# Converting float64 weights on the fly: a mask that also sets a bit, and the sign put into the power, in a recurrence with an MLP

## The chip, the cores and the metric

The kernel runs on one core of a Trainium2 chip. The metric is the device time of one execution in microseconds. The core has five engines with instruction streams of their own, each in program order: TensorE (PE in the profile; its weight loads are PEld), VectorE (DVE), ScalarE (ACT), GpSimd (POOL) and SyncE (SP), which here mostly issues DMA transfers. They wait for one another by semaphores.

## The reference

Two blocks, one after the other. The first is a recurrence over 768 steps for 4 batches and 8 heads with a state of 40 x 40; the second an MLP whose activation is h cos h:

```
for t in range(S):
    y[:, :, t] = np.einsum('bhd,bhde->bhe', rt, state)
    Sa = np.einsum('bhde,bhe->bhd', state, at)
    state_decay = state * wt[:, :, None, :] - np.einsum('bhd,bhe->bhde', Sa, bt)
    state = state_decay + np.einsum('bhd,bhe->bhde', vt, kt)
...
x = attn_out.transpose(0, 2, 1, 3).reshape(B * S, H * D)    # 3072 x 320
h = x @ w_in                                                # 320 x 2048
g = h * np.cos(h)
return (g @ w_out).astype(np.float32)                       # 2048 x 320
```

The inputs of the recurrence are float32. The two weights of the MLP come as float64, since a float32 array times a float64 scalar gave that in the set-up. [...]

## The kernel before, in words

**The recurrence** is worked in 24 chunks of 32 steps (`NCH`), with the four batches on the 128 partitions. For each chunk there is preparation of the decays (`p1_w`, `p1_a`, `p1_b`, `p1_n`), an inverse of a small triangular matrix for every group of four chunks (for the first eight chunks by blocks, `pair_first`, `pair_second`), preparation of keys, values and queries (`p2_in`, `p2_kn`, `p2_v`, `p2_k`, `p2_g`) and the chain from state to state (`main`: `ch_t`, `ch_q`, `ch_x`, `ch_s`, `ch_z`). `ch_z` ends with four pairs of VectorE operations (qz L738, yt L745), four products on GpSimd (qz L739) and one more (yt L750). The yt tile goes to DRAM and comes back transposed as xT (`tokens`, L759 to L771).

**The MLP** runs over pairs of chunks, 256 tokens each, in pieces: `first_a` and `first_b` multiply xT with w_in into ph, L812 to L822 form the cosine and the product gT, `second` multiplies gT with w_out into po.

**The order** of all this is written out by hand. `step` emits one segment, then those works put off with `later` that have come due, then a stated number of entries of two lists: `inv_steps` (the inverse) and `w_steps` (the weights). Each engine executes what it was given in just this order. Where TensorE would fall idle early in the kernel, `busy` and `kept_busy` put matmuls of zeros (tiles busy, spare).

**The weights** are cut into 20 pieces of 128 x 512 values: 8 of w_in_sb, 2 of w_in_tail and 10 of w_out_sb. Each piece has four works, made by `rounded`:

- `fetch` (L233 to L237) loads the piece as pairs of 32-bit words into a tile `words`, low word first, high word second, so either word is read with a stride of two. The tile shares the buffers of other things (gT, nt, u, inv).
- `taken` (L239 to L249): VectorE masks the upper 20 bits of the mantissa out of the high word (mant, L243) and shifts the exponent down (expo, L244). ScalarE moves the exponent to its float32 place with Relu (L247) and takes the sign of the high word (sign, L249).
- `mantissa` (L251 to L256): VectorE adds the low word times 2^-32 to the masked bits (L253). ScalarE brings the sum to a fraction with the leading 1 and a constant factor by Identity with a scale and a bias (L256).
- `product` (L258 to L262): VectorE multiplies fraction and power (the exponent's bits read as float32) into the weight's place (L259). GpSimd multiplies that with the sign (L262).

The constant factors fold 1/(2 pi) into w_in and 2 pi into w_out; they are held per partition in by_in and by_out.

The list `w_steps` is built at L921 to L930: first `taken` of pieces 0 and 1 and `mantissa` of piece 0, and then for every piece n its `product`, the `fetch` of a later piece, `mantissa` of n + 1 and `taken` of n + 2. So `taken` of a piece comes ahead of the product of the piece before it, and mant, expo and sign have two buffers each (pool `sb2`). The list is emptied between 48 and 143 us: two or four entries beside a segment for chunks 0 and 1, then two or three; a piece of the MLP that needs weights not yet converted takes further entries first (`piece`, L1020).

Of the kernel before, what the change touches and what calls it, by code (L numbers as in the profile page):

```python
# [9 lines left out]
F32 = mybir.dt.float32  # L10
I32 = mybir.dt.int32
U32 = mybir.dt.uint32
ALU = mybir.AluOpType
ACTF = mybir.ActivationFunctionType
# [6 lines left out]
def kernel(  # L21
# [43 lines left out]
    nc = tc.nc  # L65
    B, H, S, D = r.shape
    P, C, DP = 128, 32, 64
# [12 lines left out]
    const = ctx.enter_context(tc.tile_pool(name="const", bufs=1))  # L80
    ring = ctx.enter_context(tc.tile_pool(name="ring", bufs=7))
    sb1 = ctx.enter_context(tc.tile_pool(name="sb1", bufs=1))
    sb2 = ctx.enter_context(tc.tile_pool(name="sb2", bufs=2))
# [6 lines left out]
    def kept(name, shape, n=1, fill=None, part=lambda t: t, on=nc.gpsimd):  # L90

        tiles = []
        for i in range(n):
            t = const.tile(shape, F32, tag=f"{name}{i}", name=f"{name}{i}")
            if fill is not None:
                on.memset(part(t), fill)
            tiles.append(t)
        return tiles
# [8 lines left out]
    src = {"r": r, "k": k, "v": v, "w": w, "a": a, "b": b}  # L107
# [12 lines left out]
    for n, fill in (("w", 1.0), ("a", 0.0), ("b", 0.0)):  # L120
        for i in range(4):
            x = slice((i - 2) * H * DP, (i - 1) * H * DP)
            if i < 2:
                t = const.tile([P, H, DP], F32, tag=f"nat_{n}{i}", name=f"nat_{n}{i}")
            else:
                t = {
                    "w": w_in_sb[:, 0, late:], "a": w_in_sb[:, 1, late:], "b": late_out
                }[n][:, x].rearrange("p (h d) -> p h d", h=H)
# [4 lines left out]
    for n in "kvr":  # L133
        t = const.tile([P, H, D], F32, tag=f"nat_{n}", name=f"nat_{n}")
# [71 lines left out]
        nc.gpsimd.memset(bn_b[i][:, :, C // 2 : C], 0.0)  # L206
    kn_b = kept("kn", [P, H, DP], 2, 0.0, padding)

    by_in = kept("by_in", [P, 1], 1, 0.5 / math.pi)[0]
    by_out = kept("by_out", [P, 1], 1, 2.0 * math.pi)[0]  # L210
    to_bits = kept("to_bits", [P, 1], 1, (127.0 - 1023) * 2**23)[0]


# [5 lines left out]
    WID = 512  # L219
    first_done, second_done = [], []  # L220

    def rounded(m, dst, src, by, by_sb):

        pool, tag = (
            ((sb2, "gT"), (sb2, "gT"), (sb1, "nt"), (sb1, "u"), (sb1, "inv"))[m % 5]
            if m < 10 else ((sb1, "nt"), (sb1, "u"), (sb1, "inv"))[(m - 10) % 3]
        )
        t = {}  # L230

        def fetch():
            t["words"] = pool.tile([P, WID, 2], I32, tag=tag, name="words")  # L233
            for rows, cols, part in src:
                nc.sync.dma_start(
                    t["words"][rows, cols].rearrange("p n w -> p (n w)"), part.bitcast(I32)
                )  # L237

        def taken():  # L239
            hi = t["words"][:, :, 1]  # L240
            t["mant"] = sb2.tile([P, WID], I32, tag="mant", name="mant")
            t["expo"] = sb2.tile([P, WID], I32, tag="expo", name="expo")
            nc.vector.tensor_scalar(t["mant"], hi, 0xFFFFF, None, ALU.bitwise_and)  # L243
            nc.vector.tensor_scalar(  # L244
                t["expo"], hi, 20, 0x7FF, ALU.logical_shift_right, ALU.bitwise_and
            )
            nc.scalar.activation(t["expo"], t["expo"], ACTF.Relu, bias=to_bits, scale=2.0**23)  # L247
            t["sign"] = sb2.tile([P, WID], mybir.dt.bfloat16, tag="sign", name="sign")
            nc.scalar.activation(t["sign"], hi, ACTF.Sign)  # L249

        def mantissa():  # L251
            frac = t["mant"].bitcast(F32)
            nc.vector.scalar_tensor_tensor(  # L253
                frac, t["words"][:, :, 0].bitcast(U32), 2.0**-32, t["mant"], ALU.mult, ALU.add
            )
            nc.scalar.activation(frac, frac, ACTF.Identity, bias=by_sb, scale=2.0**-20 * by)  # L256

        def product():  # L258
            nc.vector.tensor_tensor(  # L259
                dst, t["mant"].bitcast(F32), t["expo"].bitcast(F32), ALU.mult  # L260
            )
            nc.gpsimd.tensor_tensor(dst, dst, t["sign"], ALU.mult)  # L262

        return fetch, taken, mantissa, product

    def weights():


        wide = moe_w_in.dtype != F32
        work = []  # L270

        def put(dst, src, by, by_sb):
            if wide:
                work.append(rounded(len(work), dst, src, by, by_sb))
                return

            def fetch():
                for rows, cols, part in src:
                    nc.sync.dma_start(dst[rows, cols], part)

            none = lambda: None
            work.append((fetch, none, none, lambda: nc.scalar.mul(dst, dst, by)))

        flat_out = w_out_sb.rearrange("p f n -> p (f n)")
        for j in range(NF // 4):
            cs = slice(j * WID, (j + 1) * WID)
            for i in range(2):
                put(
                    w_in_sb[:, i, cs], [(every, slice(0, WID), moe_w_in[i * P : (i + 1) * P, cs])],
                    0.5 / math.pi, by_in,  # L290
                )
            if j % 2 == 0:
                put(
                    w_in_tail[:, j : j + 2].rearrange("p j f n -> p (j f n)"),
                    [
                        (
                            full[e], slice(2 * i * P, 2 * (i + 1) * P),
                            moe_w_in[2 * P :, (4 * (j + i) + 2 * e) * P : (4 * (j + i) + 2 * e + 2) * P],
                        )
                        for i in range(2)  # L300
                        for e in range(2)
                    ],
                    0.5 / math.pi, by_in,
                )
            first_done.append(len(work))
            for o in range(0, NF * DM, WID):
                if not 4 * j * DM <= o < 4 * (j + 1) * DM:
                    continue
                parts = []
                for f in range(o // DM, (o + WID - 1) // DM + 1):  # L310
                    lo, hi = max(o, f * DM), min(o + WID, (f + 1) * DM)
                    parts.append(
                        (
                            every, slice(lo - o, hi - o),
                            moe_w_out[f * P : (f + 1) * P, lo - f * DM : hi - f * DM],
                        )
                    )
                put(flat_out[:, o : o + WID], parts, 2.0 * math.pi, by_out)
            second_done.append(len(work))
        return work  # L320

# [582 lines left out]
    def main(c):  # L904
        def last():
            ch_z(c)
            if c + 2 < NCH:
                later(8 if c == 2 else 1, lambda: p2_kn(c + 2))

        return [lambda: ch_t(c), lambda: ch_q(c), lambda: ch_x(c), lambda: ch_s(c), last]  # L910

    with tc.manual_schedule():

        w_work = weights()
        w_count = [0]

# [116 lines left out]
        for c in range(NCH):  # L1033
            t, q, x, s, z = main(c)
# [116 lines left out]
```

## Time and profile before

| | us |
|---|---|
| median of 4 runs | 809.18 (806.14 to 812.27) |
| the execution that was profiled | 809.11 |
| its span, first to last instruction | 807.4 |

| engine | busy us | share of the span |
|---|---|---|
| PE (matmuls) | 754.7 | 93% |
| PEld (weight loads) | 579.5 | 72% |
| DVE | 486.6 | 60% |
| ACT | 387.6 | 48% |
| POOL | 200.7 | 25% |

The span is cut into 40 slices of 20.2 us; each digit is a busy share in tenths. The conversion of the weights lies in slices 3 to 8.

```profile
PE   3867898989999999999999999999999999999997
DVE  6968958864744896553894645994346763333231
ACT  1336567555435436535535635534545445354352
POOL 5316625230321330330330230332032122201000
PEclk9888799999999999999999999999999999999999
```

PEclk is the TensorE clock that was granted, in tenths of full speed. A group of instructions is told by its line, engine, operation, tile and shape, with its count, its busy time, the mean duration of one in ns and the idle time of its engine just ahead of it, with what ended that. Busy PE time includes the matmuls of zeros.

### The profile page before, as it was taken

What the parts mean: (1) busy time and instruction counts of PE and PEld (TensorE: products, weight loads), DVE (VectorE), ACT (ScalarE), POOL (GpSimd) and SP (SyncE); (2) the same over time, 40 slices, a digit from 0 to 9 for tenths busy, and PEclk for the clock granted to TensorE, in tenths of its full rate; (3) what the DMA queues carried; (4) which work ended last, traced back from release to release, by engine and by line L of the source; (5) the groups of instructions that cost most, each with busy time, mean ns of one, the idle gap of its engine ahead of it and who ended that gap; (6) DMA issues with size and microseconds to landing.
All of it is one profiled execution on the core that took longest, in us unless ns stands there. A gap on an engine that the chain in (4) does not pass through costs nothing.

```text
span 807.4 us, 39677 instructions
## 1 busy us (share of the span) xinstructions
PE 754.7 (93%) x17859; PEld 579.5 (72%) x17859; DVE 486.6 (60%) x1025; ACT 387.6 (48%) x723; POOL 200.7 (25%) x354
## 2 busy tenths in 40 slices
PE   3867898989999999999999999999999999999997
PEld 2635477767777777777777787777787777777775
DVE  6968958864744896553894645994346763333231
ACT  1336567555435436535535635534545445354352
POOL 5316625230321330330330230332032122201000
PEclk9888799999999999999999999999999999999999
DMA  7477552343253314324214323223120222001000
GB/s 124 74 193 217 141 136 77 59 118 67 56 124 66 65 36 70 90 75 68 57 39 68 88 44 72 45 50 72 37 47 19 46 46 53 20 15 36 19 17 16
DMA packets 183304, 55.79 MB, mean 69 GB/s; under 512 B 157152, under 2 KB 178656, under 8 KB 183136
## 3 DMA queue, kind: packets, MB, share of 16 engines
q1 hardware_dynamic: 180560, 51.95, 29.4%
q8 instruction: 140, 2.29, 1.1%
q10 hardware_dynamic: 2320, 0.98, 0.6%
q0 software_dynamic: 256, 0.33, 0.2%
q14 instruction: 28, 0.23, 0.1%
HBM read 42.07 MB, written 11.14 MB: 66 GB/s over the span
## 4 chain that ended last, share of the span: by engine, by line
PE 66%; DVE 14%; DMA 5%; SPq 4%; issue 4%; ACT 4%; POOL 3%; DVEq 0%; POOLq 0%; ACTq 0%
PE ph L101 23%; PE po L101 19%; SPq L152 4%; PE x0ps L101 3%; PE dps L101 3%; PE gram L101 3%; DVE rw L393 3%; PE vT L328 2%; DVE inv_tmp L480 2%; DVE inv L484 2%; PE sps L101 2%; PE qps L101 2%; PE nps L101 1%; DMA xd<-yt 1%; PE kT L328 1%
## 5 line engine op out<-in xcount | busy, mean ns | idle before, releaser
L101 PE MATMUL po<-w_out_sb,gT 128*128 128x320 f32 x768 | 223.2, 439 | 0.0
L101 PE MATMUL ph<-xT,w_in_sb 128*128 128x256 f32 x768 | 185.4, 386 | 0.9 <-DMA xT<-xd 0.5
L101 PEld LDWEIGHTS po<-w_out_sb,gT 128*128 128x128 f32 x768 | 140.2, 190 | 54.2 <-issue 1.7
L101 PEld LDWEIGHTS ph<-xT,w_in_sb 128*128 128x128 f32 x768 | 139.3, 190 | 29.7 <-issue 11.6
L812 ACT ACTIVATE turns<-ph,rnd 128x512 f32<-128x512 f32 x96 | 64.3, 686 | 159.5 <-PE ph L101 159.1
L814 DVE SCALAR_TENSOR_TENSOR turns<-turns,ph 128x512 f32<-128x512 f32 x96 | 64.1, 684 | 112.1 <-ACT turns L812 111.8
L822 DVE TENSOR_TENSOR gT<-ph,turns 128x512 f32<-128x512 f32 x96 | 65.9, 687 | 38.9 <-ACT turns L819 38.9
L739 POOL TENSOR_TENSOR qz<-qz,wc 128x160 f32<-128x160 f32 x92 | 42.2, 476 | 177.3 <-DVE qz L738 176.5
L819 ACT ACTIVATE turns<-turns,half_pi 128x512 f32<-128x512 f32 x96 | 69.4, 723 | 3.1
L818 ACT ACTIVATE turns<-turns 128x512 f32<-128x512 f32 x96 | 60.2, 627 | 17.5 <-DVE turns L814 17.5
L101 PE MATMUL ph<-xT,w_in_tail 64*128 64x256 f32 x384 | 55.6, 402 | 1.6 <-issue 1.2
L484 DVE TENSOR_TENSOR inv<-inv,inv_tmp 128x31 f32<-128x31 f32 (+15 forms) x124 | 50.5, 408 | 4.3
L738 DVE TENSOR_TENSOR qz<-dps,qz 128x160 f32<-128x160 f32 x92 | 29.2, 317 | 38.3 <-PE dps L101 38.0
L572 POOL COPY vp<-nat_v 128x320 f32<-128x320 f32 x24 | 12.3, 513 | 155.1 <-DMA nat_v<-in_v_dram 143.8
L480 DVE TENSOR_TENSOR inv_tmp<-u,inv 128x31 f32<-128x31 f32 (+15 forms) x124 | 48.9, 394 | 2.3
L393 DVE RECIPROCAL rw<-nat_w 128x320 f32<-128x320 f32 x20 | 42.9, 2143 | 0.0
L644 ACT COPY s<-sT 128x512 f32<-128x512 f32 x46 | 24.5, 584 | 35.9 <-PE sT L640 35.8
L101 PEld LDWEIGHTS ph<-xT,w_in_tail 64*128 64x128 f32 x384 | 33.5, 186 | 11.4 <-issue 7.7
L101 PEld LDWEIGHTS <-idle 32*64 32x64 bf16 (+2 forms) x443 | 20.6, 98 | 23.4 <-issue 17.3
L750 POOL TENSOR_TENSOR yt<-yt,wb 128x512 f32<-128x512 f32 x24 | 31.6, 1318 | 22.4 <-DVE yt L745 22.4
L704 DVE TENSOR_TENSOR sm<-sps,su 128x128 f32<-128x128 f32 x48 | 11.7, 286 | 32.4 <-ACT sm L699 29.6
L394 POOL TENSOR_TENSOR bn<-nat_b,rw 128x320 f32<-128x320 f32 x22 | 20.1, 912 | 43.4 <-DVE rw L393 41.1
(136 smaller groups left out, 1123.8 us busy)
## 6 DMA issues: line engine op xcount, KB each, us to landing
words<-in_moe_w_in_dram SPq DMA_DIRECT2D x8, 512.0 KB
nat_k<-in_k_dram SPq DMA_DIRECT2D x96, 40.0 KB
nat_v<-in_v_dram SPq DMA_DIRECT2D x96, 40.0 KB
nat_r<-in_r_dram SPq DMA_DIRECT2D x96, 40.0 KB
xd<-yt SPq DMA_DIRECT2D x48, 80.0 KB
out_dram<-ot SPq DMA_DIRECT2D x24, 160.0 KB
nat_b<-in_b_dram SPq DMA_DIRECT2D x88, 40.0 KB
nat_a<-in_a_dram SPq DMA_DIRECT2D x80, 40.0 KB
```

The costliest lines, as they stand in the source:

```text
L101: nc.tensor.matmul(o, lhsT=lhsT, rhs=rhs, start=start, stop=stop, skip_group_check=True)
L152: via.dma_start(nat[n, c][blk[i], :, :D], at_c.rearrange("h t d -> t h d"))
L393: nc.vector.reciprocal(rw, wn)
L480: nc.vector.tensor_tensor(tmp, u[:, j : j + 1, :j].to_broadcast([P, C - j, j]), x[:, j:, j : j + 1].to_broadcast([P, C - j, j]), ALU.mult,)
L484: nc.vector.tensor_tensor(x[:, j:, :j], x[:, j:, :j], tmp, ALU.subtract)
L739: nc.gpsimd.tensor_tensor(z, z, wc.rearrange("p (f m b) -> p f m b", f=2, m=2)[:, :, :, bb] .unsqueeze(3).to_broadcast([P, 2, 2, D]), ALU. ...
L750: nc.gpsimd.tensor_tensor(yt.rearrange("p j b t -> p (j b) t"), yt.rearrange("p j b t -> p (j b) t"), wx, ALU.mult)
L812: nc.scalar.activation(n, u, ACTF.Identity, bias=rnd, scale=1.0)
L814: nc.vector.scalar_tensor_tensor(n, n, -ROUND, u, ALU.add, ALU.subtract)
L818: nc.scalar.activation(n, n, ACTF.Abs)
L819: nc.scalar.activation(n, n, ACTF.Sin, bias=half_pi, scale=-2.0 * math.pi)
L822: nc.vector.tensor_tensor(gT[:, 2 * e : 2 * e + 2].rearrange("p f t -> p (f t)"), us[e], ns[e], ALU.mult)
```

## The change

One constant takes the place of two: a column of the integer 2^20 (the bit above the 20 of the mask), set once by GpSimd. In each of the 20 pieces:

- The mask moves from `taken` to `mantissa`. There, one VectorE operation of a scalar and two tensors takes the bits of the high word by the mask and sets bit 20 from the constant, repeated along the row: the leading 1 is now in the integer.
- The sum with the low word stays. The Identity pass on ScalarE is gone.
- The constant factor and 2^-20 go into the product, which becomes an operation of a scalar and two tensors as well: mantissa times factor times power.
- The sign is multiplied into the power, on GpSimd still, in `taken`. The multiplication of the finished weight is gone.
- On ScalarE the sign is taken ahead of Relu.

```
-    by_in = kept("by_in", [P, 1], 1, 0.5 / math.pi)[0]
-    by_out = kept("by_out", [P, 1], 1, 2.0 * math.pi)[0]
+    one = const.tile([P, 1], I32, tag="one", name="one")
+    nc.gpsimd.memset(one, 1 << 20)
...
         def taken():
             hi = t["words"][:, :, 1]
-            t["mant"] = sb2.tile([P, WID], I32, tag="mant", name="mant")
             t["expo"] = sb2.tile([P, WID], I32, tag="expo", name="expo")
-            nc.vector.tensor_scalar(t["mant"], hi, 0xFFFFF, None, ALU.bitwise_and)
+            t["sign"] = sb2.tile([P, WID], mybir.dt.bfloat16, tag="sign", name="sign")
             nc.vector.tensor_scalar(
                 t["expo"], hi, 20, 0x7FF, ALU.logical_shift_right, ALU.bitwise_and
             )
+            nc.scalar.activation(t["sign"], hi, ACTF.Sign)
             nc.scalar.activation(t["expo"], t["expo"], ACTF.Relu, bias=to_bits, scale=2.0**23)
-            t["sign"] = sb2.tile([P, WID], mybir.dt.bfloat16, tag="sign", name="sign")
-            nc.scalar.activation(t["sign"], hi, ACTF.Sign)
+            power = t["expo"].bitcast(F32)
+            nc.gpsimd.tensor_tensor(power, power, t["sign"], ALU.mult)
 
         def mantissa():
+            t["mant"] = sb2.tile([P, WID], I32, tag="mant", name="mant")
             frac = t["mant"].bitcast(F32)
             nc.vector.scalar_tensor_tensor(
+                t["mant"], t["words"][:, :, 1], 0xFFFFF, one.to_broadcast([P, WID]),
+                ALU.bitwise_and, ALU.bitwise_or,
+            )
+            nc.vector.scalar_tensor_tensor(
                 frac, t["words"][:, :, 0].bitcast(U32), 2.0**-32, t["mant"], ALU.mult, ALU.add
             )
-            nc.scalar.activation(frac, frac, ACTF.Identity, bias=by_sb, scale=2.0**-20 * by)
 
         def product():
-            nc.vector.tensor_tensor(
-                dst, t["mant"].bitcast(F32), t["expo"].bitcast(F32), ALU.mult
-            )
-            nc.gpsimd.tensor_tensor(dst, dst, t["sign"], ALU.mult)
+            nc.vector.scalar_tensor_tensor(
+                dst, t["mant"].bitcast(F32), 2.0**-20 * by, t["expo"].bitcast(F32), ALU.mult, ALU.mult
+            )
```

The rest of the diff only drops the argument `by_sb` from `rounded`, `put` and their calls. The order of the works in `w_steps` is the same.

More of the change, by code (lines that the diff above doesn't have):

```diff
@@ L220, with rounded @@
     first_done, second_done = [], []
-    def rounded(m, dst, src, by, by_sb):
+    def rounded(m, dst, src, by):
         pool, tag = (
@@ L270, in weights, with put @@
         work = []
-        def put(dst, src, by, by_sb):
+        def put(dst, src, by):
             if wide:
-                work.append(rounded(len(work), dst, src, by, by_sb))
+                work.append(rounded(len(work), dst, src, by))
                 return
@@ L289, in weights @@
                     w_in_sb[:, i, cs], [(every, slice(0, WID), moe_w_in[i * P : (i + 1) * P, cs])],
-                    0.5 / math.pi, by_in,
+                    0.5 / math.pi,
                 )
@@ L302, in weights @@
                     ],
-                    0.5 / math.pi, by_in,
+                    0.5 / math.pi,
                 )
@@ L317, in weights @@
                     )
-                put(flat_out[:, o : o + WID], parts, 2.0 * math.pi, by_out)
+                put(flat_out[:, o : o + WID], parts, 2.0 * math.pi)
             second_done.append(len(work))
```

## The prediction
> **What bounds the kernel now.** I read the stages first (busy time of each engine in stretches cut at places where VectorE falls idle), then the groups of the conversion, then the chain of work that ended last, then the instructions in order of time in the tightest stretch. The stages, columns PE, PEld, DVE, ACT, POOL, granted clock, DMA share, GB/s:
>
> ```profile
> 47.00:63.40 16.40, 10.03 (x339) 5.95 (x339) 8.24 (x24) 6.09 (x12) 3.58 (x5) 0.74 0.70 185
> 63.40:79.20 15.80, 13.49 (x465) 9.24 (x464) 15.77 (x21) 12.50 (x22) 11.39 (x11) 0.93 0.73 209
> 79.20:93.60 14.40, 9.38 (x257) 5.49 (x257) 11.15 (x27) 7.99 (x15) 6.68 (x8) 0.78 0.49 120
> 93.60:101.80 8.20, 7.82 (x164) 5.45 (x165) 8.17 (x10) 5.88 (x11) 6.95 (x8) 0.79 0.50 154
> 101.80:128.30 26.50, 24.88 (x752) 19.41 (x750) 15.54 (x38) 18.60 (x34) 8.70 (x12) 1.00 0.48 130
> 128.30:145.90 17.60, 16.63 (x288) 13.60 (x288) 16.61 (x22) 11.07 (x19) 9.53 (x13) 1.00 0.20 52
> ```
>
> All 20 pieces of weight are converted between 48 and 143 us. VectorE is full in three of these stretches (15.77 of 15.80, 8.17 of 8.20, 16.61 of 17.60) and has idle time in the others (8.2, 3.2 and 11.0 us). After 146 us no conversion is left: TensorE is busy 198 of 200 us in the middle of the run. So the change can only bring the start of that steady part forward or push it back, and an arrival shifted by x shifts the end by about x. The groups of the conversion, with mean ns:
>
> ```profile
> L243 DVE TENSOR_SCALAR mant<-words 128x512 int32<-128x512 int32 x20 | 17.0, 850 | 0.1
> L253 DVE SCALAR_TENSOR_TENSOR mant<-words,mant 128x512 f32<-128x512 uint32 x20 | 15.6, 782 | 0.0
> L247 ACT ACTIVATE expo<-expo,to_bits 128x512 int32<-128x512 int32 x20 | 14.5, 724 | 9.5 <-DVE expo L244 9.3
> L262 POOL TENSOR_TENSOR w_out_sb<-w_out_sb,sign 128x512 f32<-128x512 f32 x10 | 13.1, 1307 | 21.3 <-DVE w_out_sb L259 14.0 <-ACT expo L247 7.3
> L244 DVE TENSOR_SCALAR expo<-words 128x512 int32<-128x512 int32 x20 | 10.5, 525 | 0.0
> L256 ACT ACTIVATE mant<-mant,by_out 128x512 f32<-128x512 f32 x10 | 7.2, 723 | 4.5 <-DVE mant L253 4.4
> L259 DVE TENSOR_TENSOR w_out_sb<-mant,expo 128x512 f32<-128x512 f32 x10 | 6.9, 686 | 1.0 <-ACT mant L256 1.0
> ```
>
> L256 is the pass that goes; ScalarE waits for VectorE before it far longer than VectorE waits after it. And L243 has a mean of 850 ns where its shortest is 414. Why, the order of time shows (VectorE, then GpSimd):
>
> ```profile
> 70.37 0.68 DVE L259 TENSOR_TENSOR w_out_sb<-mant,expo 128x512 f32<-128x512 f32 x1
> 70.97 0.68 DVE L253 SCALAR_TENSOR_TENSOR mant<-words,mant 128x512 f32<-128x512 uint32 x1
> 71.58 1.38 DVE L243 TENSOR_SCALAR mant<-words 128x512 int32<-128x512 int32 x1
> 72.88 0.41 DVE L244 TENSOR_SCALAR expo<-words 128x512 int32<-128x512 int32 x1
> ...
> 71.13 1.54 POOL L262 TENSOR_TENSOR w_out_sb<-w_out_sb,sign 128x512 f32<-128x512 f32 x1 [0.96 <-DVE w_out_sb L259]
> ```
>
> GpSimd's sign operation is asked for at 71.13, lasts 1.54 instead of the 1.16 us of its shortest, and ends at 72.67; L243, issued at 71.58, ends 0.29 us after it. The two engines take turns. It isn't L243 alone: L253 started at 131.69, inside the sign operation of 131.25 to 132.41, and took 1.26 us; L259 started at 95.63, inside the yt product of 95.39 to 96.84, and took 1.76. Operations with a PSUM source don't wait (L738 stays at 0.32 beside qz products).
>
> **The change part by part.** A slot is the distance from one start to the next when VectorE is full: 0.60 us for L259 and L253 (70.37, 70.97, 71.58), 0.34 for an unblocked L243 or L244 (48.54, 48.88, 49.21).
> *Taken away on ScalarE:* 20 x 0.722 = 14.4 us of busy time. On VectorE's path it is worth little: the product waited for it 1.9 us in all, three times. On ScalarE's own path it moves later copies (sm, vvm, turns) forward by one slot, 0.63 us (120.27 to 120.90), where they wait for ScalarE and not for TensorE.
> *The mask,* L243, becomes an operation of two tensors with a scalar. No row has a bitwise one. Bounds: below, L244's unblocked slot, 0.34; above, the longest L253, 1.35. I take L253's 0.60, the same form at the same width, one source with the same stride of two words. A source that repeats one element costs nothing in the inverse: L480, with such a source, has a median of 368 ns, L484 of the same sizes without 390. So +0.26 a tile against an unblocked L243.
> The Trainium skill (Vector Engine (DVE) Microarchitecture Reference, Points that are easy to get wrong) speaks against this: such an operation with two SBUF sources that aren't bf16 is said to run at half throughput. By that rule, as an estimate from the same page's 1.04 ns a column (Measured stream behaviour on trn2), mask, sum and product would each take some 0.5 us more, 30 us of VectorE in all. L253 is such an operation and takes 684 ns beside the 686 of L259, so the row is against the rule, and the row stands.
> *The sum* stays. *The product* goes from a tensor product (686 ns) to L814's form (684): nothing.
> *The sign* stays on GpSimd with the same shapes, so 1.16 us, but works on the power, right after Relu, and before the product instead of behind it. VectorE's product now waits for GpSimd where it waited for ScalarE. What queues behind it on VectorE is the next mask, sum and exponent, and qz, gT or sm. It is emitted two pieces ahead of where it was, so Relu (0.66) and the sign (1.16) have the previous product, the mask, the sum and the next exponent, 0.60 + 0.60 + 0.60 + 0.34 = 2.14 us, to hide behind. If that cover failed, a product would wait up to 1.16 us.
> *Sign ahead of Relu on ScalarE:* nothing while the sign pass (0.55 slot) runs under VectorE's exponent; where ScalarE is late it delays Relu by 0.55, and the slack of 2.14 - 0.66 - 1.16 covers 0.32 of that.
> *No DMA, fetch or load moves:* each buffer of words is still last read by the sum; SP was already held at L235 by it (19.7 us, 7 times). One constant of GpSimd less at the start, outside the chain.
>
> Now the sum, by stretch. In 63.4 to 79.2 a full tile is now 0.60 + 0.60 + 1.30 + 0.34 = 2.84 us (starts 70.37, 73.21, 76.05). After it is 3 x 0.60 + 0.34 = 2.14 plus one turn of GpSimd, 1.30 - 0.34 = 0.96: 3.10, so +0.26 for 5 tiles, **+1.3**. In 79.2 to 93.6 the chain goes through ScalarE four times (Identity L256, Relu, sign, sm, to 89.07); two Identity slots fewer give 1.3 back: **-1.3**. There the product of piece 9, then qz and yt, start when they did. In 93.6 to 101.8 two more tiles, +0.5, run out into the 1.95 us idle before L553: **0**. To 128.3 TensorE is the bound. In 128.3 to 145.9 VectorE is the chain: one exponent less ahead of the first product (L243 at 128.89 waited for yt, the exponent now does: -0.2), two full tiles +0.5, and the last piece loses 0.85 of waiting for ScalarE but takes a mask of 0.60 and GpSimd's bn product (0.86 when alone), which had run under that wait: +0.2 to +0.8. I take **+0.5**.
> The execution profiled took 809.11 us with a span of 807.4, 1.7 around it; it lies 0.07 below the median of the four runs. The span becomes 807.9, the time 809.6, against the median **809.7**.
>
> **The rivals.** *GpSimd gets out of the way (faster).* If the sign falls into VectorE's idle or PSUM operations, a full tile costs 2.14 instead of 2.84: -0.70 for 5 tiles, about -0.5 each for 2 of the three in the last stretch: -4.5, **804.7**. For it: the sign starts at another time, after Relu. Against it: in a full stretch VectorE has three two-tensor operations and a scalar one in each cycle, and none leaves GpSimd a gap.
> *The mask is slow (slower).* If its slot is 1.22, twice L253's, VectorE loses a further 0.62 a tile. Nine tiles to 93.6: 5.6, less the 3.2 idle of 79.2 to 93.6, is +2.4; the two after run into idle; three in the last stretch +1.9: with my +0.5 that makes +4.8, **814.0**. For it: no row has a bitwise operation of two tensors. Against it: L243 and L244 do their bit operations at twice the rate of L253. It leaves the half per cent (4.05 us) from a slot of about 1.1.
> *It does not do what it says:* the waits only change their name and every stretch is as long as it was, 809.2; this can't be told from my forecast, and is counted with it.
>
> **How the numbers follow.** Half a per cent is about what a measurement of this kernel can tell from no change (its four runs span 806.1 to 812.3). Forecast with its twin 0.50, own range 806 to 813; faster rival 0.20; slow mask 0.24; 0.06 for a shift of TensorE's clock or of its fetching gaps ("issue" is 8.7% of the chain in the first 300 us), half of it on either side. The split is then 0.23 faster, 0.50 same, 0.27 slower. The range takes most of both rivals: 804.5 to 815.
>
> **What would show it.** Right: the mask at 0.68 us when alone; VectorE's busy time in the conversion within 5 us of before; exponent operations of over 1.2 us where masks had them; ScalarE 14 us less busy; VectorE waiting under 2 us for GpSimd before the product; sm of piece 9 near 89 us, the yt store near 97. Wrong if the mask is over 1 us alone (slow rival), if full tiles come every 2.2 us (faster rival), or if products wait for GpSimd by a microsecond each, which would put the conversion's end beyond 143 us by more than 4.

## The result, and the profile after

The changed kernel takes 813.01 us (median of 46 runs, 808.08 to 821.85) against 809.46 for the kernel before (72 runs). The ratio is **1.0046** with a 95% interval of 1.0034 to 1.0058: slower by 2.8 to 4.7 us, 3.7 in the middle. The middle is just inside the half per cent that counted as no change, the upper end outside it. The time lies inside the range given, but the loss is seven times the 0.5 us that were forecast. The execution profiled took 810.85 us with a span of 808.4, so it is one of the quicker ones, and times of single events are read from it with care.

Line numbers of the changed kernel: exponent L243, sign pass L246, Relu L247, GpSimd's sign L249, mask L254, sum L258, product L263. Its busy time in the stretches that the prediction used (columns as there):

```profile
47.00:63.40 16.40, 11.84 (x472) 7.43 (x473) 12.77 (x26) 4.98 (x11) 5.03 (x6) 0.79 0.69 189
63.40:79.20 15.80, 13.58 (x463) 8.46 (x462) 15.63 (x20) 9.81 (x17) 11.24 (x11) 0.91 0.64 178
79.20:93.60 14.40, 10.98 (x255) 6.65 (x256) 12.22 (x25) 5.99 (x12) 5.88 (x7) 0.62 0.62 154
93.60:101.80 8.20, 6.42 (x149) 4.46 (x150) 8.13 (x12) 3.98 (x8) 8.20 (x9) 1.00 0.43 137
101.80:128.30 26.50, 24.12 (x781) 18.78 (x770) 21.26 (x38) 17.00 (x30) 9.00 (x11) 0.99 0.49 133
128.30:145.90 17.60, 17.60 (x288) 14.24 (x288) 17.39 (x23) 7.56 (x13) 7.74 (x12) 0.92 0.21 57
```

The bounds are those of the kernel before, so work that came later counts in a later row. VectorE has gained busy time wherever it had room (12.77 where it had 8.24, 21.26 where it had 15.54), and GpSimd is full between 93.6 and 101.8 (8.20 of 8.20). ScalarE is relieved in every stretch. The groups of the conversion:

```profile
L258 DVE SCALAR_TENSOR_TENSOR mant<-words,mant 128x512 f32<-128x512 uint32 x20 | 23.4, 1169 | 0.7
L254 DVE SCALAR_TENSOR_TENSOR mant<-words,one 128x512 int32<-128x512 int32 x20 | 17.0, 852 | 0.0
L243 DVE TENSOR_SCALAR expo<-words 128x512 int32<-128x512 int32 x20 | 11.6, 584 | 1.7 <-DMA words<-in_moe_w_out_dram 1.5 <-DMA words<-in_moe_w_in_dram 0.2
L249 POOL TENSOR_TENSOR expo<-expo,sign 128x512 f32<-128x512 f32 x20 | 26.0, 1304 | 45.6 <-ACT expo L247 45.6
```

The mask costs no more busy time than it did (17.0 us both times; its median is 684 ns). The sum has grown from a mean of 782 ns to 1169: it is now the operation that waits for GpSimd. One piece in the full stretch, VectorE first, then GpSimd:

```profile
71.10 0.68 DVE L263 SCALAR_TENSOR_TENSOR w_out_sb<-mant,expo 128x512 f32<-128x512 f32 x1
71.70 0.69 DVE L254 SCALAR_TENSOR_TENSOR mant<-words,one 128x512 int32<-128x512 int32 x1
72.42 1.52 DVE L258 SCALAR_TENSOR_TENSOR mant<-words,mant 128x512 f32<-128x512 uint32 x1
73.87 0.41 DVE L243 TENSOR_SCALAR expo<-words 128x512 int32<-128x512 int32 x1
74.20 0.68 DVE L263 SCALAR_TENSOR_TENSOR w_out_sb<-mant,expo 128x512 f32<-128x512 f32 x1
...
72.01 1.39 POOL L249 TENSOR_TENSOR expo<-expo,sign 128x512 f32<-128x512 f32 x1 [1.12 <-ACT expo L247]
```

A piece comes every 3.10 us (71.10, 74.20), where it came every 2.84. GpSimd asks at 72.01 while the mask runs, gets its turn when the mask is done, ends at 73.40, and the sum ends 0.54 later. The mask's own slot is 0.72, not 0.60: the sum reads its result, so it starts 0.03 behind the mask's end instead of 0.08 ahead of it.

### The profile page after: what moved, and what is told of

The parts are those of the page before. It is cut to its first block, busy times and chain, and to the rows that moved or that the text cites. A ratio compares the mean times of both kernels' runs of the same rounds, so it can differ in the third digit from the quotient of the medians.

```text
span 808.4 us, 39629 instructions
## 1 busy us (share of the span) xinstructions
PE 758.0 (94%) x17859; PEld 580.8 (72%) x17859; DVE 496.9 (61%) x1025; ACT 375.2 (46%) x703; POOL 202.0 (25%) x353
## 4 chain that ended last, share of the span: by engine, by line
PE 67%; DVE 16%; DMA 5%; issue 4%; ACT 3%; SPq 3%; POOL 2%; DVEq 0%; POOLq 0%; ACTq 0%
PE ph L101 24%; PE po L101 19%; PE x0ps L101 4%; PE dps L101 3%; DVE rw L396 3%; PE gram L101 3%; DVE inv_tmp L483 2%; PE vT L331 2%; DVE inv L487 2%; PE sps L101 2%; PE nps L101 2%; PE qps L101 2%; SPq L152 2%; DMA xd<-yt 1%; PE sT L643 1%
## 5 line engine op out<-in xcount | busy, mean ns | idle before, releaser
L249 POOL TENSOR_TENSOR expo<-expo,sign 128x512 f32<-128x512 f32 x20 | 26.0, 1304 | 45.6 <-ACT expo L247 45.6
```

## The experiments

Three theories stood against each other. **V**: VectorE's slots. The mask costs a full slot where a scalar operation cost 0.34, so the full stretches are longer. **S**: the mask ahead of the sum releases the words later; SP holds the next fetch, and the store of yt and the loads queue behind it. In the profile after, the fetch of piece 7 indeed ran on SP at 66.37 instead of 64.49, and the first xd store behind it at 66.79 instead of 65.58. **G**: GpSimd's sign stands ahead of qz and yt in its order. Each kernel was timed beside runs of the kernel before on the same chip; ratios are against those.

**Only the place of the mask undone.**

```diff
         def taken():
+            (mant allocated, mask by scalar_tensor_tensor)
             (expo, Sign, Relu, sign into the power)
         def mantissa():
-            (mant allocated, mask by scalar_tensor_tensor)
             (sum)
```

> The changed kernel with its mask (the same operation of a scalar and two tensors) back in taken, ahead of the exponent, so that mantissa holds the sum alone. Theory S (the mask ahead of the sum releases the words later, SP holds the next fetch, and xd and the loads queue behind it): the sum comes back to its old place, xd of the first chunk to about 65.7 us, the time to a ratio of 1.000 to 1.002 against the kernel before. Theory V (VectorE's slots: the mask costs 0.6 to 0.7 us where it cost 0.34, so full stretches are longer): the work is the same, ratio 1.004 to 1.005. Theory G (GpSimd's sign now stands ahead of qz and yt): ratio 1.004 to 1.005.

Ratio 1.0019 (0.9995 to 1.0044). A full piece still comes every 3.10 us: without the dependence the mask's slot is 0.60 when alone, but with GpSimd's turn in it 1.57. V's expectation of 1.004 to 1.005 is touched only by the interval's upper end, and "nothing" lies inside as well. So the run alone tells little, and it was made again, after all the runs that follow here:

> e1_mask_early once more, for its interval. Theory V by the slots seen: a free mask costs 0.60 us there, 0.26 more than by two scalars, and not the 0.72 it takes ahead of a sum that waits for its result; 20 pieces at the 0.5 to 0.6 that f1_mask_twice and f2_after_sum show to arrive at the end give 2.6 to 3.1 us, ratio 1.003 to 1.004, between e3_two_scalars and the changed kernel. The form costs nothing and only the place does: 0.999 to 1.001.

Ratio 1.0031 (1.0004 to 1.0058). That leaves out a ratio of 1.000 exactly, but "the form costs nothing" was given up to 1.001, which the interval touches. In this run the first xd store started at 65.72 us, as S wanted. The two runs lie at 1.002 and 1.003, between a cheap mask and the changed kernel, as V has it by the revised slot; how much of the difference to the changed kernel is real they don't settle.

**The sign back behind the product.**

```diff
         def taken():
-            nc.scalar.activation(t["sign"], hi, ACTF.Sign)
             (Relu)
-            nc.gpsimd.tensor_tensor(power, power, t["sign"], ALU.mult)
+            nc.scalar.activation(t["sign"], hi, ACTF.Sign)
         def product():
             (product)
+            nc.gpsimd.tensor_tensor(dst, dst, t["sign"], ALU.mult)
```

> The changed kernel with the sign again multiplied into the finished weight by GpSimd behind the product, and Relu ahead of the sign on ScalarE. Theory G: ratio back to 1.000 to 1.001. Theories S and V: stays at 1.004 to 1.005.

Ratio 1.0016 (0.9991 to 1.0040), a full piece every 3.10 us. This is inconclusive: its upper end touches what V and S expect, its middle lies nearer to G. The next pair answers it for a cheap mask only.

**The mask by two scalars,** then the same with the sign in its old place as well.

```diff
         def taken():
+            nc.vector.tensor_scalar(t["mant"], hi, 0xFFFFF, 1 << 20, ALU.bitwise_and, ALU.bitwise_or)
         def mantissa():
-            (mask by scalar_tensor_tensor)
```

> The changed kernel with the mask in taken and done by an operation of two scalars on one tensor (and with the mask, or with 2^20). Theory V: 0.34 us a slot again, a full tile 2.84 us, ratio 0.998 to 1.000. Theory S: the same, since the sum is back in its place. Theory G: stays at 1.003 to 1.005. Beside e1_mask_early it gives the price of the form of the mask alone: by V 0.003 to 0.005, by S and G under 0.002.

> The kernel before without its pass on ScalarE and nothing else moved: mask by two scalars in taken, factor in the product, sign by GpSimd behind the product, Relu ahead of the sign. It is e3_two_scalars with the sign in its old place. Theory V: a full piece every 2.84 us as before, ratio 0.998 to 1.000, as e3_two_scalars. Theory G (the sign's place costs): 0.002 or more below e3_two_scalars, so under 0.998.

Ratios 0.9997 (0.9971 to 1.0023) and 1.0004 (0.9976 to 1.0031). In both a full piece comes every 2.84 us again (74.86 and 77.71 in the one, 71.29 and 74.13 in the other). The operation does the same work as the changed kernel's mask, without a second tensor. So the loss goes with the mask's slot, and G alone falls: with a cheap mask, the sign ahead of the product is no slower than behind it. The price of the mask's form alone, e1_mask_early less e3_two_scalars, is 0.002 by the first run and 0.003 by the second; V wanted 0.003 to 0.005, S and G under 0.002, and the intervals leave both. The second kernel is the kernel before without its pass on ScalarE and nothing else moved: taking that pass away brought nothing that can be seen.

**The fetch of piece 7 behind the first xd store.**

```diff
+            if n == 3:
+                w_steps.append(w_work[7][0])
-            if nxt < len(w_work):
+            if nxt < len(w_work) and n != 2:
                 w_steps.append(w_work[nxt][0])
```

> The changed kernel with the fetch of piece 7 handed to SP one product later, behind the xd store of the first chunk. Theory S: xd starts at the end of yt (about 65.8 us) instead of 66.8, ratio 1.001 to 1.003. Theories V and G: stays at 1.004 to 1.005.

Ratio 1.0041 (1.0017 to 1.0065). The store started at 65.69, as S wanted, and the time stayed. The late store that the profile shows is real, and nothing shows that the kernel pays for it, though the upper part of S's range lies inside the interval.

On the same chip, this kernel's 12 runs lie 2.5 us (1.0 to 3.9) above the 24 of e1_mask_early and e2_sign_last together, by their means. All three have a full piece of 3.10 us. So the length of a full piece may not be the whole loss: with the costlier mask, taking either of the other two moves back (the mask's place, the sign's place) seems to save a part. The second run of e1_mask_early, on another chip, shows less of that. Which of the two it is, or both, was not taken apart.

**One more VectorE operation in each piece,** once ahead of the sum (the mask twice), once behind it.

```diff
         def mantissa():
             (mask)
+            (mask once more)                                                         # mask twice
             (sum)
+            nc.vector.scalar_tensor_tensor(frac, frac, 1.0, frac, ALU.mult, ALU.max) # behind the sum
```

> The changed kernel with its mask done twice, so one more operation of 0.6 to 0.7 us on VectorE in each piece, ahead of the sum. Theory V (VectorE's slots): going from a mask of two scalars to the changed kernel added 0.26 us a full piece and 0.4 to 0.5 per cent, so this adds about 1 per cent to the changed kernel: ratio 1.012 to 1.016, a full piece every 3.7 to 3.8 us. Theory S (words released late): more than f2_after_sum by at least 0.003. If VectorE's slots were hidden: 1.005 to 1.007.

> The changed kernel with one more operation of the same form on VectorE in each piece behind the sum (it keeps the larger of the fraction and itself), so that the words are released when they were. Theory V: as f1_mask_twice, ratio 1.012 to 1.016. Theory S: 1.005 to 1.010, at least 0.003 less than f1_mask_twice.

Ratios 1.0141 (1.0100 to 1.0182) and 1.0153 (1.0110 to 1.0196); a full piece every 3.82 and 3.83 us. The one that releases the words late is not the slower one by its middle, and the other lies above all that S allowed it (1.005 to 1.010). So S falls in this form, and V gets a price. Against the changed kernel they add 0.72 and 0.73 us a full piece, 14.6 us over the 20 pieces, and 0.95 and 1.07 per cent of 809.5 us, 7.7 and 8.7 us: **between a half and six tenths of VectorE's extra time arrives at the end** (with some 3.5 us of uncertainty on either side, so 0.3 to 0.8).

**The sign on VectorE.** The mask by two scalars, no GpSimd operation in the conversion.

```diff
         def taken():
-            nc.gpsimd.tensor_tensor(power, power, t["sign"], ALU.mult)
         def product():
+            nc.vector.tensor_tensor(power, power, t["sign"], ALU.mult)
             (product)
```

> e3_two_scalars with the sign multiplied into the power on VectorE, in product, and no GpSimd operation in the conversion. If the turns that VectorE and GpSimd take are what a full piece pays for, a piece comes every 0.34 + 0.34 + 0.60 + 0.72 + 0.60 = 2.6 us instead of 2.84, ratio 0.995 to 0.999. If the turns cost nothing, VectorE has 0.72 us more in each piece: ratio 1.005 to 1.010.

The order of time of this kernel on VectorE:

```profile
74.10 0.69 DVE L262 SCALAR_TENSOR_TENSOR w_out_sb<-mant,expo 128x512 f32<-128x512 f32 x1
74.70 0.69 DVE L255 SCALAR_TENSOR_TENSOR mant<-words,mant 128x512 f32<-128x512 uint32 x1
75.31 0.42 DVE L242 TENSOR_SCALAR mant<-words 128x512 int32<-128x512 int32 x1
75.64 0.42 DVE L247 TENSOR_SCALAR expo<-words 128x512 int32<-128x512 int32 x1
75.98 0.68 DVE L261 TENSOR_TENSOR expo<-expo,sign 128x512 f32<-128x512 f32 x1
76.70 0.69 DVE L262 SCALAR_TENSOR_TENSOR w_out_sb<-mant,expo 128x512 f32<-128x512 f32 x1
```

A piece every 2.60 us, no operation over 0.69: an operation added to VectorE makes it quicker than GpSimd's turn did. But the ratio is 1.0003 (0.9976 to 1.0030). In its profile VectorE waits 3.1 us for the words of a w_in piece, where the kernel before waits for none (e3_two_scalars, at 0.9997, waits 3.7). Those words stand behind loads in SP's queue, so the loads were moved, in this kernel, in the kernel before and in the changed one:

```diff
-        for n, c, name in ((3, 4, "w"), (5, 5, "w"), (7, 5, "b")):
+        for n, c, name in ((11, 4, "w"), (12, 5, "w"), (13, 5, "b")):
```

> e6_sign_on_vector with twelve loads of the fourth and fifth chunk (two of w, one of b) handed to SP 6 to 8 segments later, behind the fetches of pieces 10 and 11. Theory L (a conversion faster than 2.84 us a piece only waits for words that stand behind these loads in SP's queue): VectorE's wait for words before piece 10, 3.1 us, falls under 1 us, ratio 0.994 to 0.998. If the words are not what holds it: 0.999 to 1.002, as e6_sign_on_vector.

> The kernel before with the same loads handed over later. VectorE waits for no words there, so by theory L and by V alike nothing is to be had: ratio 0.998 to 1.001. Under 0.997 would mean that the queue of loads bounds the kernel before as well.

> The changed kernel with the same loads handed over later. Theory V (its loss is VectorE's slots): stays at 1.003 to 1.006, and 0.003 to 0.006 above g2_before_later. Theory S in its wider form (its loss is the words' lateness in SP's queue, of which VectorE and ScalarE waited 0.2 and 2.5 us before piece 10): 1.000 to 1.002.

Ratios 1.0000 (0.9974 to 1.0026), 1.0017 (0.9990 to 1.0045) and 1.0047 (1.0020 to 1.0073). In the first the wait of 3.1 us went away (1.0 us for words of w_out is left), and no gain can be seen: theory L fails here. The second lies above what was expected, and its VectorE waits 2.4 us for words of a w_out piece, where the kernel before waits for none. In the third the wait before piece 10 is gone and the loss stays, at 1.0047 and 0.003 above the second, so that wait is not its cause. But VectorE waits 2.8 us there for words of a w_out piece (1.5 us for such words without the move), so the run does not clear the words' lateness as a whole. It does speak against another cause that the prediction gave a chance: the granted TensorE clock has a mean of 0.978 over its runs and 0.977 over those of the kernel before.

## Why the prediction was right or wrong

**The full piece: right to 0.01 us.** 3.10 us were forecast and 3.10 measured. Its parts were off and cancelled: the mask's slot is 0.72 for its dependence, GpSimd's turn costs 0.85 instead of 0.96. The Trainium skill (SBUF — State Buffer, SBUF: two separate sides) has VectorE and GpSimd hold a shared pair of ports in turn for a whole instruction, where VectorE reads two SBUF tensors or runs in a two-port mode. The trace agrees: the sum of two tensors takes 1.52 us beside GpSimd's product, where it takes 0.69 alone (its shortest; the same operation before the change has a median of 0.68).

**The mask's price: right.** 684 ns at its median, as L253's row said; the rule that such an operation runs at half throughput does not hold for it here.

**What of it is hidden: wrong, and this is the step that failed.** The sum by stretch had +1.3, **-1.3**, **0**, 0 and +0.5. VectorE shows them in the profiles, by the starts of four operations: the rt that ends the first stretch, the second chunk's sm, the rt that should follow the idle time of the third, and the aT behind the last product. Before, then after:

```profile
78.89 0.27 DVE L553 TENSOR_TENSOR rt<-rt,below 128x128 f32<-128x128 f32 x1
89.07 0.49 DVE L704 TENSOR_TENSOR sm<-sps,su 128x128 f32<-128x128 f32 x2 [0.90 <-ACT sm L699]
103.72 0.29 DVE L553 TENSOR_TENSOR rt<-rt,below 128x128 f32<-128x128 f32 x1 [1.95 <-PE below L101]
141.37 1.28 DVE L399 TENSOR_TENSOR aT<-aps,wb 128x512 f32<-128x512 f32 x2
```

```profile
80.42 0.27 DVE L556 TENSOR_TENSOR rt<-rt,below 128x128 f32<-128x128 f32 x1
89.46 0.49 DVE L707 TENSOR_TENSOR sm<-sps,su 128x128 f32<-128x128 f32 x2 [0.56 <-ACT sm L702]
104.96 0.27 DVE L556 TENSOR_TENSOR rt<-rt,below 128x128 f32<-128x128 f32 x1
142.87 1.28 DVE L402 TENSOR_TENSOR aT<-aps,wb 128x512 f32<-128x512 f32 x2
```

*The first term* held: rt is 1.5 late, and 0.2 of that was there when the stretch began.

*The second* came in part, and for another reason. At sm 1.1 us had been given back. The prediction put that down to two Identity passes fewer, and put the sign's place on ScalarE at nothing. The kernel e5_scalar_only has no Identity pass either, and its sign pass is still behind Relu:

```profile
79.81 0.27 DVE L554 TENSOR_TENSOR rt<-rt,below 128x128 f32<-128x128 f32 x1
89.99 0.49 DVE L705 TENSOR_TENSOR sm<-sps,su 128x128 f32<-128x128 f32 x2 [1.17 <-ACT sm L700]
```

From rt to sm it takes 10.18 us, as long as the kernel before; the changed kernel takes 9.04, and e3_two_scalars, with the sign ahead of Relu, 8.26. So the Identity passes gave nothing back here. The sign pass did: it no longer stands between Relu and the copies (x, vvm, sm) that VectorE waits for. On ScalarE, before and then after:

```profile
79.69 0.64 ACT L249 ACTIVATE sign<-words 128x512 bf16<-128x512 int32 x1
80.24 0.38 ACT L681 COPY x<-x0ps 128x288 f32<-128x288 f32 x1
```

```profile
80.53 0.72 ACT L247 ACTIVATE expo<-expo,to_bits 128x512 int32<-128x512 int32 x1 [1.80 <-DVE expo L243]
81.16 0.38 ACT L684 COPY x<-x0ps 128x288 f32<-128x288 f32 x1
```

That the term was nearly right at sm is luck. Behind sm the cost came on again: the second chunk's first qz started 1.0 late (92.83 against 91.80), where the prediction had qz and yt start when they did.

*The third,* 0, failed: rt came 1.2 late, with no idle time left before it. The xd store came 2.1 late (98.92 against 96.86): 1.0 from qz, 0.3 since GpSimd finished its sign operation later ahead of the qz products, and 0.7 since its four qz products took 2.79 us instead of 2.35 and yt 1.71 instead of 1.45, beside masks and sums of two tensors that take turns with them.

*The fourth and fifth:* by 123 us VectorE was level again (rt at 123.05 against 123.18); its next qz, which waited for TensorE, came 0.7 late (127.25 against 126.56), and aT 1.5 late, so the last stretch cost 0.8 and not 0.5.

That is one execution, whose span is 1.0 longer; over many the loss is 3.7, and which stretch makes up the rest is not shown. The runs put a price in place of the five terms: 0.53 and 0.59 of the time of an operation added to VectorE in the conversion arrives (0.3 to 0.8 with the intervals). With +0.26 a piece that makes 20 x 0.26 x 0.53 = 2.8 us, with the +0.38 that a mask with its dependence costs against an unblocked one 20 x 0.38 x 0.59 = 4.5. The measured 2.8 to 4.7 fit, though with so wide a price this is no sharp test. In the profiles of f1_mask_twice and f2_after_sum the conversion itself is longer: from the first chunk's first qz to the last product 89.0 and 91.3 us, against 80.3 in the changed kernel and 79.0 before. And the shift is carried through as the prediction had it: the seventh x (259.91 us before) is 16.2 and 17.3 late, the end of the span 15.2 and 18.5. So the mechanism (slots, turns, a steady part that starts later) was right, and the terms that made the cost vanish were not: the sum is too small by a factor of seven.

**Product waits for GpSimd: right.** VectorE waits nowhere for the sign; the 2.14 us of cover held.

**No fetch moves: wrong, at no price that was seen.** The fetch of piece 7 and the first xd store on SP did go late, by 1.9 and 1.2 us: the sum still is the last to read the words, but it comes behind the mask now. Taking the store's lateness away gained nothing that can be seen. VectorE also waits 1.7 us for words in the profile after, where it waited for none; what that costs was not settled.

**ScalarE's pass: right that it is worth little.** ScalarE has 12.4 us less of busy time (387.6 to 375.2; 14.4 were forecast), and e5_scalar_only shows no gain. But the second term had counted on it for 1.3.

**What was named to look for:** sm came near 89 us, but the xd store at 98.9 and not near 97. In a full piece the wait sits in the sum, not in the exponent operation. VectorE's busy time rose by 10.3 us (486.6 to 496.9), twice the 5 us that were given as the limit.

**The rivals.** GpSimd did not get out of the way: a full piece never came every 2.2 us. Where VectorE took over its work, the conversion got quicker and the kernel didn't, so this rival's price of 4.5 us looks too high as well. The slow mask did not come; its price, 4.3 us for 0.62 a piece, was too low by the number above (20 x 0.62 x 0.53 = 6.6).

**Open:** why no gain is seen from time taken from VectorE below 2.84 us a piece, where time added does arrive. At the price above it would be 2.5 us (20 x 0.24 x 0.53), a ratio of 0.997, just below the intervals of both kernels with the sign on VectorE (from 0.9976 and 0.9974); at the price's lower end, 0.3, it would lie inside them. Moving the loads did not bring it out. In the profile of the second of these kernels TensorE waits 1.9 us for xT and some microseconds for nothing that the profile shows; neither was tried. Open too is why e1_mask_early and e2_sign_last, with the changed kernel's full piece, seem to lose less than it.

No version tried beats the kernel before.

## What to carry to other kernels

VectorE was full in stretches of 41.6 us out of 98.9. The gaps of an engine between such stretches don't simply swallow what is added to it: price an added operation by doubling it on the chip, not by filling the gaps on paper. A mask that must also set a bit can do both with two scalars on one tensor; given a second tensor, it costs a full slot instead of half of one (0.60 us and more against 0.34 here). A pass taken from an engine that waits for its producer, as ScalarE did here, need not bring anything. What stands between a pass and the copy that another engine waits for can matter more: here the sign pass, put one place forward.

## What the runs showed of the hardware

Replacing a 1.16 us GpSimd operation by a 0.68 us VectorE operation shortened a piece on VectorE itself, 2.84 to 2.60 us, since VectorE stood still through GpSimd's turn. And an operation that reads the result of the one before it starts 0.03 us behind that one's end, one that doesn't 0.08 ahead: 0.12 us for a dependence at 512 columns, seen twice: mask and sum in the changed kernel, sign and product where VectorE does both (75.98 and 76.70).
